# Window attention with keys on partitions and a mask table after exp, ahead of a routed expert layer

## The chip, the cores and the metric

The kernel runs on one core of one Trainium2 chip. The metric is device time in microseconds (us) of one execution; three runs of the kernel before gave 893.92, 901.37 and 901.82 us, a median of 901.37 us. One execution was also recorded by the hardware profiler. Its rows name the engines: PE is TensorE's matmuls, PEld its weight loads, DVE VectorE, ACT ScalarE, POOL GpSimd, SP SyncE; a q behind a name means the engine's own queue, as it issues a DMA. L310 is line 310 of the kernel.

## What is computed

```python
# attention: q, k, v are (4 batches, 8 heads, 768 tokens, 64), n_global = 8, n_local = 96
scores = (1 / 8) * q @ k.T                       # per batch and head
rel = pos[:, None] - pos[None, :]
is_global = pos[None, :] < n_global
is_local = (rel >= 0) & (rel < n_local)
dist = where(is_global & ~is_local, n_local, abs(rel))
scores = where(is_global | is_local, scores - slope[h] * dist, -1e9)
a = exp(scores - max(scores)); a = a / (sum(a) + 1e-9)
x = concat_heads(a @ v)                          # (3072 tokens, 512)
# router and experts: 8 experts, w1 (512, 1024), w2 (1024, 512)
logits = normalised(x) @ normalised(expert_emb).T / tau
e = argmax(logits); gate = softmax(logits)[e]
out = gate * (relu(x @ w1[e]) @ w2[e])           # each token by its one expert
```

A query sees the 96 keys up to itself and the first 8 keys of the sequence. Each token goes to one expert. All data are float32.

## The kernel before

The kernel has two stages. `window_attention` (L256) computes attention and routes tokens; then a loop over the eight experts (L616) gathers each expert's tokens from DRAM, runs two matmul layers over up to 512 token slots and scatters the result to the output.

Before attention, `load_numbers` (L62) reads n_global and n_local and forms a flag that says whether the window fits. `values_load` (L606) brings it to the engines' registers and a `tc.If` chooses between `window_attention` and `dense_attention`. `window_bias` (L203) builds on DVE a bias for each head: minus slope times distance for a kept key, -1e9 for another.

Attention works on units: a pair of heads (2a, 2a + 1) and two tiles of 128 queries, 48 units in all. For each pair of heads `load` (L268) issues six DMAs for q, k and v on SP's queue, two pairs ahead, and POOL copies v into `vb`, whose first 32 rows are the sequence's first values (L278, L279). `prep` (L285) transposes six tiles of q and six of k (L291) and copies them to `qT` and `kT`. Then

- `score` (L303) multiplies with queries stationary, 64 rows deep (one head on partitions 0 to 63, the other on 64 to 127), 256 keys moving (L310). DVE scales and adds the bias (L315) and takes the maximum (L321); ACT computes exp with the maximum taken off and sums it (L326).
- `turn` (L329) transposes the weights (L336), so that keys lie on partitions, and ACT copies them out (L338).
- `attend` (L341) multiplies with the weights stationary, 128 by 128, and 64 columns of values moving (L348, L350). DVE divides by the sum (L352 to L354).

In the loop at L377 the score of unit i stands beside the turn of unit i - 1 and the attend of unit i - 2. The program is handed to a scheduler that orders each engine's instructions, so neighbouring steps can stand in one another.

When a batch's last unit is attended, `finish` (L359) writes its x to DRAM and calls `route` (L126) for six tiles of 128 tokens: squares for the norm (L131), four transposes per tile (L140), a copy (L142), four matmuls of 8 columns against the expert embedding (L145), and for the whole batch the choice of the expert, the gate and each token's slot (L149 to L192), then six indirect DMAs on POOL that scatter token number and gate into `meta` (L194). All six write the same tensor, so each waits for the one before. The weights of the first two experts are loaded after batch 0.

`expert` (L492) loads its slots (L495), gathers token rows by indirect DMA (L502), transposes them (L508) and multiplies (L517, L524). `overflow` (L534) handles an expert with more than 512 tokens; here it has nothing to do.

Of the kernel before, what the change touches and what calls it, by code (L numbers as in the profile page):

```python
# [9 lines left out]
F32 = mybir.dt.float32  # L10
# [6 lines left out]
P = 128  # L17
NEG = 1e9
GR = 32  # rows of a "before" key block that hold the sequence's first keys instead
CAP = 512  # token slots of one pass through an expert  # L20
# [6 lines left out]
def build_consts(k):  # L27
    nc, pool = k.nc, k.const
    k.ident = pool.tile([P, P], F32, name="ident")
    make_identity(nc, k.ident[:])  # L30

    # prefix[k, m] = 1 where k < m
# [4 lines left out]
    k.ones = pool.tile([P, P], F32, name="ones")  # L37
    nc.vector.memset(k.ones[:], 1.0)
    k.half = pool.tile([P, k.NT], F32, name="half")
    nc.vector.memset(k.half[:], 0.5)  # L40

# [7 lines left out]
    nc.vector.memset(k.cnt[:], 0.0)  # L49

    # A slot that no token takes names the row of zeros behind the last token, with gate 0.
    cols = k.E * k.N // P
    fill = k.setup.tile([P, cols, 2], F32, name="fill")
    nc.vector.memset(fill[:, :, 0], float(k.N))
    nc.vector.memset(fill[:, :, 1], 0.0)
    nc.scalar.dma_start(k.meta[:].rearrange("(p c) w -> p c w", p=P), fill[:])
    zrow = k.setup.tile([1, k.DM], F32, name="zrow")
    nc.vector.memset(zrow[:], 0.0)
    nc.scalar.dma_start(k.x_dram[k.N : k.N + 1, :], zrow[:])


def load_numbers(k, n_global, n_local):  # L62
    """n_global and n_local as float32 on every partition, and whether the windowed path holds."""
    nc, pool = k.nc, k.const
    raw = pool.tile([P, 2, 2], I32, name="raw")
    for i, ap in enumerate((n_global, n_local)):
        nc.sync.dma_start(raw[:, i, :], ap.bitcast(I32).partition_broadcast(P))
# [9 lines left out]

    ok = pool.tile([P, 3], F32, name="ok")
    nc.vector.tensor_scalar(out=ok[:, 0:1], in0=k.ng, scalar1=float(GR), scalar2=None, op0=ALU.is_le)
    nc.vector.tensor_scalar(out=ok[:, 1:2], in0=k.nl, scalar1=float(P - GR + 1), scalar2=None,  # L80
                            op0=ALU.is_le)
    nc.vector.tensor_scalar(out=ok[:, 2:3], in0=k.nl, scalar1=1.0, scalar2=None, op0=ALU.is_ge)
    flag = pool.tile([P, 1], F32, name="flag")
    nc.vector.tensor_reduce(out=flag[:], in_=ok[:], op=ALU.min, axis=AX.X)
    k.flag_i = pool.tile([P, 1], I32, name="flag_i")
    nc.vector.tensor_copy(out=k.flag_i[:], in_=flag[:])


def prep_expert_emb(k, emb_in, tau):
# [27 lines left out]
def new_weights(k):  # L117
    w1 = k.wp.tile([P, k.NC, k.F], F32, name="w1t", tag="w1t")
    w2 = k.wp.tile([P, k.NF, k.DM], F32, name="w2t", tag="w2t")
    return w1, w2  # L120


# [1 line left out]


def route(k, b, xb, pool):  # L126
# [525 lines left out]
```

## Time and profile before

| what | value |
|---|---|
| median of three runs | 901.37 us |
| span of the profiled execution, first to last instruction | 891.9 us |
| PE busy | 776.3 us, 87% of the span |
| PEld, DVE, ACT, POOL busy | 465.0, 243.8, 233.6, 130.4 us |
| first score matmul | 22.52 us |
| last block of attention normalised | 344.29 us |
| first expert matmul | 412.16 us |
| moved by DMA | 74.31 MB |
| granted TensorE clock, mean | 0.894 of 2.4 GHz |

The profiled execution's span is 9.5 us below the median of the runs. Busy time is the time in which an engine has an instruction in hand; matmuls overlap, and their ends are modelled, so records close behind each other share time. A float32 matmul call shows as two records, a transpose as one. Times of rows count from the span's start.

### The profile page before, as it was taken

Reading aid. Unit: us, or ns where it says so; the run is one execution under the profiler, and the core shown is the slowest. Engines: PE = TensorE matmul, PEld = TensorE weight load, DVE = VectorE, ACT = ScalarE, POOL = GpSimd, SP = SyncE. Lnnn points to the kernel's source line nnn. Section 1 sums busy time; section 2 is a strip of 40 time slices with the busy share of each in tenths; the row PEclk is TensorE's granted clock in tenths of the full one; section 3 lists DMA queues with packets and bytes.
Section 4 is the critical chain, followed back from the end, with each engine's and each line's share of the span. In section 5 each row is a group of like instructions: output and inputs, shape, how many; then the busy total and the mean of one; then the engine's idle time right before and its main releaser. Section 6 shows DMA issues by size and latency. Waiting matters only on the chain. (4 is left out here: it accounts for less than half of the span.)

```text
span 891.9 us, 8302 instructions
## 1 busy us (share of the span) xinstructions
PE 776.3 (87%) x3092; PEld 465.0 (52%) x3092; DVE 243.8 (27%) x562; ACT 233.6 (26%) x623; POOL 130.4 (15%) x153
## 2 busy tenths in 40 slices
PE   1899899899998997307999999999999999999993
PEld 1777687677776776303444444444444444444441
DVE  7676256624562672201011020010100101102000
ACT  1677356824573565000100001001010010000100
POOL 3110102210221020014012020020110101101000
PEclk9999569955896797556999999999999999999998
DMA  7796514531332001004114231342142412300000
GB/s 148 189 244 187 133 36 72 104 74 36 64 62 89 19 1 72 3 1 118 48 75 151 101 110 53 118 155 105 31 141 102 141 32 113 126 12 33 1 17 17
DMA packets 98498, 74.31 MB, mean 83 GB/s; under 512 B 79362, under 2 KB 79490, under 8 KB 98450
## 3 DMA queue, kind: packets, MB, share of 16 engines
q1 hardware_dynamic: 89248, 52.47, 22.1%
q0 software_dynamic: 5888, 14.71, 4.7%
q10 hardware_dynamic: 3314, 6.51, 2.0%
q8 instruction: 27, 0.44, 0.2%
q14 instruction: 21, 0.17, 0.1%
HBM read 60.87 MB, written 14.90 MB: 85 GB/s over the span
## 5 line engine op out<-in xcount | busy, mean ns | idle before, releaser
L517 PE MATMUL big<-xT,w1t 128*128 128x512 f32 x512 | 223.5, 597 | 11.2 <-DVE xT L509 10.4
L524 PE MATMUL work<-w2t,hT 128*128 128x512 f32 x512 | 221.0, 592 | 0.0
L517 PEld LDWEIGHTS big<-xT,w1t 128*128 128x128 f32 x512 | 97.3, 191 | 132.8 <-issue 120.8
L524 PEld LDWEIGHTS work<-w2t,hT 128*128 128x128 f32 x512 | 97.3, 190 | 122.5 <-issue 122.5
L519 ACT ACTIVATE hT<-big 128x1024 f32<-128x1024 f32 x32 | 32.8, 1024 | 450.8 <-PE big L517 450.8
L527 DVE TENSOR_SCALAR y<-work,emt 128x512 f32<-128x512 f32 x32 | 24.0, 750 | 385.8 <-PE work L524 385.8
L326 ACT ACTIVATE ex<-sc,nm 128x256 f32<-128x256 f32 x192 | 95.2, 499 | 15.2 <-DVE nm L321 15.1
L310 PE MATMUL big<-kT,qT 64*128 64x256 f32 x384 | 88.5, 497 | 11.4 <-DVE kT L301 9.6
L528 POOL DMA_INDIRECT out_dram<-y,ids x32 | 32.0, 1000 | 336.3 <-DVE y L527 328.6
L350 PE MATMUL work<-v,pt 128*128 128x64 f32 x384 | 74.4, 284 | 0.0
L336 PE MATMUL work<-ident,ex 128*128 128x128 f32 x352 | 66.3, 304 | 7.1 <-ACT ex L326 6.7
L315 DVE SCALAR_TENSOR_TENSOR sc<-big,bias 128x1024 f32<-128x1024 f32 x48 | 58.5, 1218 | 37.8 <-PE big L310 37.8
L348 PE MATMUL work<-vb,pt 128*128 128x64 f32 x320 | 63.4, 282 | 0.0
L350 PEld LDWEIGHTS work<-v,pt 128*128 128x128 f32 x384 | 61.2, 205 | 0.0
L338 ACT COPY pt<-work 128x512 f32<-128x512 f32 (+1 forms) x96 | 51.0, 549 | 38.9 <-PE work L336 38.0
L310 PEld LDWEIGHTS big<-kT,qT 64*128 64x128 f32 x384 | 45.4, 225 | 29.0 <-issue 19.5
L336 PEld LDWEIGHTS work<-ident,ex 128*128 128x128 f32 x352 | 43.5, 157 | 30.6 <-ACT ex L326 24.2
L321 DVE TENSOR_REDUCE nm<-sc 128x4 f32<-128x1024 f32 x48 | 58.3, 1215 | 0.4
L145 PE MATMUL work<-en,xt 128*128 128x8 f32 x192 | 43.2, 354 | 17.1 <-ACT xt L142 16.2
L145 PEld LDWEIGHTS work<-en,xt 128*128 128x128 f32 x192 | 41.0, 315 | 29.9 <-ACT xt L142 28.4
L348 PEld LDWEIGHTS work<-vb,pt 128*128 128x128 f32 x320 | 51.9, 204 | 1.0 <-ACT pt L338 1.0
L194 POOL DMA_INDIRECT meta<-mt,slot x24 | 23.7, 986 | 184.6 <-DVE slot L191 111.7
(110 smaller groups left out, 443.6 us busy)
## 6 DMA issues: line engine op xcount, KB each, us to landing
w1t<-in_moe_w_dram SPq DMA_DIRECT2D x8, 2048.0 KB
w2t<-in_moe_w_dram SPq DMA_DIRECT2D x8, 2048.0 KB, 10.3
q<-in_q_dram SPq DMA_DIRECT2D x32, 192.0 KB, 3.3
k<-in_k_dram SPq DMA_DIRECT2D x32, 192.0 KB, 5.2
v<-in_v_dram SPq DMA_DIRECT2D x32, 192.0 KB, 2.8
x_dram<-xb ACTq DMA_DIRECT2D x4, 1536.0 KB
xg<-x_dram,ids POOLq DMA_INDIRECT x32, 3.6
out_dram<-y,ids POOLq DMA_INDIRECT x32, 2.7
```

The lines of the kernel that those rows point to most:

```text
L145: nc.tensor.matmul(lp[:, 0:E], lhsT=xt[:, c, :], rhs=k.en[:, c, :], start=c == 0, stop=c == k.NC - 1)
L310: nc.tensor.matmul(sp[:, e, r, :], lhsT=t.qT[rows, 2 * g + r, :], rhs=t.kT[rows, 2 * g + r, :, :].rearrange("p i c -> p (i c)"), start=Tru ...
L315: nc.vector.scalar_tensor_tensor(out=sc[:].rearrange("p e r c -> p e (r c)"), in0=sp[:].rearrange("p e r c -> p e (r c)"), scalar=k.scale, ...
L321: nc.vector.tensor_reduce(out=nm[:], in_=sc[:], op=ALU.max, axis=AX.X, negate=True)
L326: nc.scalar.activation(u.ex[:, e, r, :], sc[:, e, r, :], AF.Exp, bias=nm[:, e, r : r + 1], accum_out=u.den[:, r, e : e + 1])
L336: nc.tensor.transpose(ps[:, i, :], u.ex[:, e, i // 2, (i % 2) * P : (i % 2 + 1) * P], k.ident[:])
L338: nc.scalar.copy(out=pt[:, first:4, :], in_=ps[:, first:4, :])
L348: nc.tensor.matmul(av[:, r, e, 0:D], lhsT=u.pts[e][:, 2 * r, :], rhs=t.vb[:, qt - 1, e, :], start=True, stop=False)
L350: nc.tensor.matmul(av[:, r, e, 0:D], lhsT=u.pts[e][:, 2 * r + 1, :], rhs=t.v[:, qt, e, :], start=qt == 0, stop=True)
L517: nc.tensor.matmul(ps[:, i, :], lhsT=w1[:, c, f * P : (f + 1) * P], rhs=xT[:, c, :], start=c == 0, stop=c == k.NC - 1)
L519: nc.scalar.activation(hT[:, 2 * f2 : 2 * f2 + 2, :], ps[:], AF.Relu)
L524: nc.tensor.matmul(ps[:], lhsT=hT[:, f, j * P : (j + 1) * P], rhs=w2[:, f, :], start=f == 0, stop=f == k.NF - 1)
```

## The change

The change replaces attention and the router's matmuls. It has these parts.

1. **Units.** A unit is now four heads (a group has two pairs of heads), one block of 96 keys, and the 192 queries that can see it (96 for the last block). There are 8 groups of 8 units. Keys are stationary: `kT[:, j]` holds block j's 96 keys and 30 first keys of the sequence, so scores come out with keys on partitions, 126 rows.
2. **No maximum, no bias.** ACT computes exp straight from PSUM. DVE multiplies the result by a table that holds exp(-slope x distance) for kept keys and 0 for others. `window_table` builds it once.
3. **Values stationary.** `attend` multiplies with 64 columns of values stationary (two heads on two halves of the output's partitions) and the weights moving; four more calls with 32 columns of ones give the sums, one head on each quarter of the output's partitions. Two blocks of keys add up in PSUM; after four blocks DVE and ACT copy three banks out (`xd`).
4. **Router from the transposed result.** `sums` multiplies `xd` by the expert embedding, 32 columns wide, and transposes logits and sums; `rows` transposes x back, scales it, stores each tile of 128 tokens on SP's queue and squares it. Both are tasks, one per unit (two near the end), that run among the next units. `choose` is the rest of the old `route`.
5. **Order and memory.** The flag and the `tc.If` at the start are gone. q, k and v are loaded two groups ahead; the first group's q goes through ACT's queue. PSUM holds one score tile, four accumulators and two banks for transposes. Only the first expert's weights are loaded during attention, the second's when attention's memory is free.
6. **Fallback at the end.** Each batch checks that its reciprocal sums lie in a range; `leftover` runs the dense path at the end where that or the fit fails. It also does what `overflow` did.

```diff
-    with tc.If(fits > 0) as arm:
+    load_numbers(n, n_global, n_local)
+    build_consts(n)
+    with ExitStack() as moe:
+        wp_a = moe.enter_context(tc.tile_pool(name="wp_a", bufs=1))
+        n.w = [new_weights(n, wp_a)]
         with ExitStack() as inner:
             window_attention(n, inner)
...
+    sp_p, od_p, tp_p = (pool("wa_sp", 1, space=PSUM), pool("wa_od", 4, space=PSUM),
+                        pool("wa_tp", 2, space=PSUM))
+    qk_p, v_p, kt_p = pool("wa_qk", 4), pool("wa_v", 3), pool("wa_kt", 4)
...
+    def turn(t, i):
+        src, half = (t.k, t.q)[i // 2], i % 2
+        ps = bank()
+        for r in range(3):
+            nc.tensor.transpose(ps[:, r * P : (r + 1) * P], src[:, 3 * half + r, :, :], k.ident[:])
...
+        if i == 1:
+            nc.gpsimd.tensor_copy(out=t.kT[:, :, BLK:ROWS],
+                                  in_=t.kT[:, 0:1, 0:GLB].to_broadcast([P, NB, GLB]))
...
+    def score(u):
+        for a in range(2):
+            t = u.g.pairs[a]
+            for e in range(2):
+                rows = slice(e * D, (e + 1) * D)
+                nc.tensor.matmul(sp[0:ROWS, e, a * n : (a + 1) * n], lhsT=t.kT[rows, j, 0:ROWS],
+                                 rhs=t.qT[rows, j * BLK : j * BLK + n], start=True, stop=True)
+        nc.scalar.activation(ex, sp[0:ROWS, :, 0 : 2 * n], AF.Exp, scale=k.scale)
+        for e in range(2):
...
+            nc.vector.tensor_tensor(out=exv, in0=exv, in1=tb, op=ALU.mult)
...
+    def attend(u):
+        for od, at, c0, c1, first in parts:
+            cols = slice(at, at + c1 - c0)
+            for a in range(2):
+                for e in range(2):
+                    nc.tensor.matmul(od[a][e * D : (e + 1) * D, cols], lhsT=g.v[0:ROWS, 2 * a + e, j, :],
+                                     rhs=ex[:, e, a * n + c0 : a * n + c1], start=first, stop=True,
+                                     skip_group_check=True)
+            for a in range(2):
+                for e in range(2):
+                    i = 2 * a + e
+                    nc.tensor.matmul(od[2][32 * i : 32 * i + 32, cols], lhsT=k.ones[0:ROWS, 0:32],
+                                     rhs=ex[:, e, a * n + c0 : a * n + c1], start=first, stop=True,
+                                     skip_group_check=True)
...
+    def sums(t, i):
+            for a in range(4):
+                nc.tensor.matmul(ps[32 * a : 32 * a + 32, 3 * P : 4 * P], lhsT=k.enb[:, a, :],
+                                 rhs=xd[a // 2][:, a % 2, c], start=True, stop=True)
+            for m in range(2):
+                nc.tensor.transpose(ps[:, m * P : (m + 1) * P], xd[m][:, 2, c], k.ident[:])
+        if i > 0:
+            nc.tensor.transpose(ps[:, 2 * P : 3 * P], t.lS[i - 1][:], k.ident[:])
...
+    def rows(t, i):
+        for a in range(4):
+            nc.tensor.transpose(ps[:, a * P : (a + 1) * P], t.groups[a // 2].xd[i // 3][:, a % 2, c], k.ident[:])
+        nc.vector.tensor_tensor(out=xs[:], in0=ps[:].rearrange("p (h d) -> p h d", d=D),
+                                in1=t.rd[:, i, :].unsqueeze(2).broadcast_to([P, H, D]), op=ALU.mult)
+        nc.sync.dma_start(k.x_dram[r0 : r0 + P, :], flat)
+        nc.scalar.activation(sq[:], flat, AF.Square, accum_out=t.ss[:, i : i + 1])
...
+    LAG = 1
+    for i in range(len(units) + LAG):
+            if u.j == 0:
+                if gi + 2 < len(groups):
+                    load(groups[gi + 2])
...
+            score(u)
+            if gi + 1 < len(groups):
+                turn(groups[gi + 1].pairs[u.j // 4], u.j % 4)
+        last = i >= len(units) - 5
+        for _ in range(2 if last else 1):
+            if tasks:
+                tasks.pop(0)()
+        if i >= LAG:
+            u = units[i - LAG]
+            attend(u)
```

## Rows read from the trace of the kernel before

**Rows 1.** windows, us: length, PE PEld DVE ACT POOL busy (records), clock, DMA share, GB/s

```profile
22.00:87.00 65.00, 59.53 (x435) 47.43 (x436) 45.17 (x78) 46.43 (x143) 10.53 (x15) 1.00 0.77 211
87.00:116.00 29.00, 25.57 (x109) 19.53 (x109) 8.41 (x21) 11.00 (x32) 3.46 (x4) 0.57 0.47 109
...
299.00:345.00 46.00, 42.96 (x330) 35.54 (x326) 28.79 (x75) 33.54 (x105) 8.03 (x9) 1.00 0.05 10
345.00:412.00 67.00, 21.24 (x88) 17.57 (x88) 9.67 (x49) 4.98 (x11) 14.15 (x15) 0.52 0.15 48
412.00:880.00 468.00, 455.45 (x1136) 207.21 (x1136) 41.68 (x66) 32.77 (x32) 55.89 (x57) 1.00 0.23 82
```

**Rows 2.** costliest groups by line: records, busy us, mean ns, idle before

```profile
L310 PE MATMUL big<-kT,qT 64*128 64x256 f32 x384 | 88.5, 497 | 11.4 <-DVE kT L301 9.6 <-ACT qT L294 1.9
L350 PE MATMUL work<-v,pt 128*128 128x64 f32 x384 | 74.4, 284 | 0.0
```

**Rows 3.** order of time on PE, 43 to 48 us: start, length, line, records

```profile
43.19 0.82 PE L291 MATMUL big<-ident,k 128*128 128x128 f32 x6
44.24 1.13 PE L310 MATMUL big<-kT,qT 64*128 64x256 f32 x8 [0.23 <-ACT qT L294]
45.30 1.34 PE L336 MATMUL work<-ident,ex 128*128 128x128 f32 x8
...
46.88 0.61 PE L350 MATMUL work<-v,pt 128*128 128x64 f32 x4
47.33 0.39 PE L348 MATMUL work<-vb,pt 128*128 128x64 f32 x2
```

**Rows 4.** order of time, the last expert's second layer on PE

```profile
864.55 13.47 PE L524 MATMUL work<-w2t,hT 128*128 128x512 f32 x31
```

**Rows 5.** order of time, the start: first q load, first scores

```profile
7.16 0.97 SPq L273 DMA_DIRECT2D q<-in_q_dram  x2
...
22.52 3.79 PE L310 MATMUL big<-kT,qT 64*128 64x256 f32 x16 [8.20 <-DVE kT L301]
```

**Rows 6.** order of time on PE while batch 0 is routed, 99 to 105 us

```profile
99.71 1.85 PE L145 MATMUL work<-en,xt 128*128 128x8 f32 x8
101.41 1.09 PE L140 MATMUL work<-ident,xb 128*128 128x128 f32 x4
102.44 1.23 PE L310 MATMUL big<-kT,qT 64*128 64x256 f32 x4
103.59 1.87 PE L145 MATMUL work<-en,xt 128*128 128x8 f32 x8
```

**Rows 7.** order of time, from the last block of attention to the first expert

```profile
344.29 0.42 DVE L354 TENSOR_TENSOR xb<-work,den 128x256 f32<-128x256 f32 x1 [1.53 <-PE work L350]
...
366.54 0.17 DVE L147 COPY lg<-work 128x8 f32<-128x8 f32 x1 [3.39 <-PE work L145]
...
372.89 1.04 POOL L194 DMA_INDIRECT meta<-mt,slot  x1 [24.94 <-DVE slot L191]
...
399.78 1.30 SPq L495 DMA_DIRECT2D emt<-meta  x3
...
412.16 3.60 PE L517 MATMUL big<-xT,w1t 128*128 128x512 f32 x4 [0.78 <-issue]
```

**Rows 8.** groups by line again, and one row of the waits

```profile
L338 ACT COPY pt<-work 128x384 f32<-128x384 f32 x32 | 15.1, 477 | 15.1 <-PE work L336 15.1
...
L294 ACT COPY qT<-big 128x768 f32<-128x768 f32 x16 | 12.8, 798 | 39.1 <-PE big L291 39.1
...
L251 DVE TENSOR_TENSOR dist<-here,rel 128x256 f32<-128x256 f32 x1 | 0.4, 420 | 0.0
...
POOL meta L194 <- DMA meta<-mt,slot: 66.1, 16, 6.2
```

More of the change, by code (lines that the diff above doesn't have):

```diff
@@ L18 @@
 NEG = 1e9
-GR = 32
 CAP = 512
+BLK = 96
+GLB = 30
+ROWS = BLK + GLB
+NB = 8
+QB = 4
+RD_LO, RD_HI = 2.0**-64, 2.0**40
 class Net:
@@ L30, in build_consts, with build_route_consts @@
     make_identity(nc, k.ident[:])
+    k.ones = pool.tile([P, P], F32, name="ones")
+    nc.vector.memset(k.ones[:], 1.0)
+def build_route_consts(k):
+    nc, pool = k.nc, k.const
     k.prefix = pool.tile([P, P], F32, name="prefix")
@@ L104, in prep_expert_emb @@
     k.en = pool.tile([P, k.NC, E], F32, name="en")
-    ps = k.work.tile([P, 512], F32, name="work", tag="work")
     for c in range(k.NC):
@@ L108, in prep_expert_emb @@
     nc.vector.tensor_copy(out=k.en[:].rearrange("p c e -> p (c e)"), in_=ps[:, 0 : k.NC * E])
+    k.enb = pool.tile([P, k.NC, 32], F32, name="enb")
+    nc.gpsimd.memset(k.enb[:], 0.0)
+    for e in range(2):
+        rows = slice(e * k.D, (e + 1) * k.D)
+        nc.gpsimd.tensor_copy(out=k.enb[rows, :, e * E : (e + 1) * E], in_=k.en[rows])
 def load_weights(k, e, w):
@@ L134, in route @@
     nc.vector.reciprocal(out=ss[:], in_=ss[:])
-    lg = pool.tile([P, NT, E], F32, name="lg", tag="lg")
-    for t in range(NT):
-        tp = k.work.tile([P, 512], F32, name="work", tag="work")
-        for c in range(k.NC):
-            nc.tensor.transpose(tp[:, c * P : (c + 1) * P], xb[:, t, c * P : (c + 1) * P], k.ident[:])
-        xt = pool.tile([P, k.NC, P], F32, name="xt", tag="xt")
-        nc.scalar.copy(out=xt[:].rearrange("p c n -> p (c n)"), in_=tp[:])
-        lp = k.work.tile([P, 512], F32, name="work", tag="work")
-        for c in range(k.NC):
-            nc.tensor.matmul(lp[:, 0:E], lhsT=xt[:, c, :], rhs=k.en[:, c, :],
-                             start=c == 0, stop=c == k.NC - 1)
-        nc.vector.tensor_copy(out=lg[:, t, :], in_=lp[:, 0:E])
     m = pool.tile([P, NT], F32, name="m", tag="m")
@@ L173, in route @@
     nc.vector.tensor_copy(out=mt[:, :, 0], in_=k.tokid[:, b * NT : (b + 1) * NT])
-    cp = k.work.tile([P, 512], F32, name="work", tag="work")
     n = NT * E
@@ new lines, in leftover @@
+    passes = -(-k.N // CAP)
+    more = passes - 1
+    flags = k.const.tile([P, 2], F32, name="flags")
+    ps = k.work.tile([P, 512], F32, name="work", tag="work")
+    nc.vector.tensor_tensor(out=k.good[:], in0=k.good[:], in1=k.fits[:], op=ALU.mult)
+    nc.tensor.matmul(ps[:, 0:1], lhsT=k.ones[:], rhs=k.good[:], start=True, stop=True)
+    nc.vector.tensor_scalar(out=flags[:, 0:1], in0=ps[:, 0:1], scalar1=float(P), scalar2=None,
+                            op0=ALU.is_lt)
+    most = k.const.tile([P, 1], F32, name="most")
@@ L614 @@
[L614 to L623 removed]
+        n.work = ctx.enter_context(tc.tile_pool(name="work", bufs=4, space=PSUM))
+        n.big = ctx.enter_context(tc.tile_pool(name="big", bufs=2, space=PSUM))
@@ L627 @@
+        wp_b = moe.enter_context(tc.tile_pool(name="wp_b", bufs=1))
+        expert_pools(n, moe)
+        for e in range(n.E):
+            if e > 0:
+                w = new_weights(n, (wp_a, wp_b)[e % 2])
+                load_weights(n, e, w)
+            else:
+                w = n.w[0]
+            expert(n, n.meta[e * n.N : e * n.N + CAP, :], *w)
+    leftover(n)
 _INS = ['q', 'k', 'v', 'n_global', 'n_local', 'moe_expert_emb', 'moe_tau', 'moe_w1', 'moe_w2']
```

510 lines of the change are left out of this document (270 added, 240 removed).

## The prediction

> **What bounds the kernel now.** I read the stretches first, then the groups of instructions, then the order of TensorE's work inside one unit, and last the two ends of attention. The stretches [rows 1] show a first part (to 345 us) in which PE is nearly always busy, a gap (345 to 412 us: PE 21 of 67 us), and the experts (412 to 880 us: PE 455 of 468 us). The diff leaves `expert` alone, so whatever the change is worth lies ahead of 412.16 us, where the first expert matmul starts [rows 7].
>
> Attention has two faces. In 22 to 87 and 299 to 345 us the clock is at its upper level of 2.4 GHz and PE is busy 92 and 93% of the time. In 87 to 116 us, where batch 0 is routed, the granted clock is 0.57 and only 109 matmul records fit in 29 us, against 435 in the 65 us before [rows 1]. That pattern comes once per batch. In it PE runs eight router records of 8 columns, four transposes, four score records, over and over, one tile per 3.9 us [rows 6]: the next batch's scores wait their turn behind the router.
>
> The groups [rows 2] say on what a unit (two heads, two query tiles) spends PE: scores (L310), transposes of the weights (L336), and weights times values with the weights stationary and only 64 columns moving (L348, L350). Those last run at 0.11 us a record (four records of L350 from 46.88 us, the next at 47.33) [rows 3], held by the weight load, not by the columns. ACT and DVE are close behind: 46.4 and 45.2 of the 65 us from 22 to 87 [rows 1].
>
> **The price of a column.** Each float32 matmul call is two records (192 calls of L310, 384 records). 31 records of L524, 512 columns each, take 13.47 us [rows 4], 0.43 us apiece, so 0.84 ns per column and record: 192 columns 0.16 us, 128 columns 0.107 us. Six transposes take 0.82 us to the end of the last, whose own length is 0.27 us: 0.11 us each [rows 3].
>
> Eight score records of 256 columns would be 1.72 us in a row, but the next work starts 1.06 us after them (44.24 to 45.30) [rows 3]. So the head on partitions 0 to 63 and the one on 64 to 127 run in pairs (4 x 0.215 = 0.86 us), and 0.2 us is left, which I charge to every change of the tile's shape.
>
> **The change, unit by unit.** 64 units now (four heads, 96 keys plus 30 global ones, 192 query columns; the last of each eight has 96). PE per full unit:
> - scores, four calls: pairs as before, 4 x 0.16 + 0.2 = 0.84 us;
> - three transposes of q or k: 0.33 us;
> - values stationary, 64 wide, heads on output partitions 0 to 63 and 64 to 127: 4 x 0.16 + 0.2 = 0.84 us if they pair, 8 x 0.16 + 0.2 = 1.49 us if not;
> - sums with 32 columns of ones, on four quarters of the output partitions: 2 x 0.16 + 0.2 = 0.52 us if four go together, 1.49 us if not.
>
> No matmul of before has a stationary operand narrower than 128, so those two prices are bounds. I take the paired one: the nearest row is the score pair, the same engine and type split along the other side. A full unit is then 2.53 us (4.15 not paired), a half one 1.73 (2.53). 56 + 8 units: 155 us (253); the unit that crosses two accumulators splits its calls, 8 x 0.4 = 3 us more. What goes: all of L336 and of L348/L350.
>
> *The Trainium skill (TensorEngine Tiling, Key Properties) says that different tiles load and multiply in parallel and that changing the tiling mode drains the engine. The score pairs agree for rows (1.06 us instead of 1.72); for columns no run here shows it. By that rule the sum is the paired one, without it the other.*
>
> The router becomes `sums` and `rows`: per tile four calls of 128 columns, 32 wide (0.21 + 0.2 us paired, 1.06 not), and seven transposes (0.77 us): 1.18 us (1.83). 21 of 24 tiles lie among units: 25 us (38). PE sums to 155 + 3 + 25 = 183 us (294); at the 93% of rows 1 that is 197 us (316).
>
> **What hides the rest.** ACT per unit: one exp of 768 columns, as L294's 0.80 us, and one 384-column copy, 0.48 us [rows 8]; with squares and evacuations some 115 us. DVE: two multiplies of 384 columns; 0.42 us for 256 [rows 8] gives about 0.56 each; with evacuations, reciprocals and scaling some 140 us. Both lie under PE's 197 us; without that cover DVE would be next. The score tile has one buffer, so the next scores wait for the exp (0.8 us); PE has transposes and the unit before (1.7 us) meanwhile. Score, exp and multiply end 3.2 us after a unit starts and its `attend` comes one unit later, so the loop can't go below some 2.1 us a unit. Loads of q, k, v (96 of 192 KB) are the same 18.9 MB; at the 211 GB/s of 22 to 87 us [rows 1] that is 89 us, still hidden. Their SP queue now also holds the row stores, which wait for DVE; two groups of prefetch cover that.
>
> **Start.** The first q load is issued at 7.16 us behind the flag's branch and the first scores run at 22.5 us [rows 5]. The branch goes, so loads leave at about 1 us; four k and q tiles, 1.57 MB, need 7.4 us at that rate; then eight copies of 0.48 us and eight table exps of the same size on ACT. I put the first unit at 16 us (13 to 22). The first 16 score records took 3.79 us [rows 5], against 1.06 for eight later: a slow beginning, 4 us.
>
> **A wait moved.** A batch's six scatters take 372.89 to 399.78 us, 27 us, each waiting on POOL for the one before (16 such waits, 66.1 us) [rows 7, 8]. The next groups' global key copies, which scores need, now stand in that same queue, as do the value copies. A group lasts some 22 us. I charge 3 us for each of three batches, 9 us; bounds 0 and 15 each. In the unpaired case a group is longer and I charge 0.
>
> **Tail.** From the last normalised block (344.29) to the first scatter (372.89) are 28.6 us [rows 7], because six tiles are routed after it. Now three are: evacuation 0.6, three tiles at 1.8 (ACT and DVE in turn), the last sums and check 2.5, then the ranks, 6.3 as from 366.54 to 372.89: about 16 us. Scatters, ids, gathers and transposes to 412.16 stay: 39.3 us. The second expert's weights now load after attention, but the first expert's 58 us cover 4.2 MB (20 us). The check at the end: 2 us.
>
> **Sum.** Last `attend` at 16 + 4 + 197 + 9 = 226 us; first expert matmul at 226 + 16 + 39.3 = 281 instead of 412.16: 131 us earlier, 129 with the end. The profiled execution's span is 891.9 us, 9.5 below the median of the runs, 901.37; I carry that difference along: 762 us of span, 772 us.
>
> **Rivals.**
> 1. Column tiles don't pair: attention ends at 16 + 4 + 316 = 336 us, experts start at 391, 19 us gained with the end: 882 us. For it: no row shows a narrow tile. Against: rows pair in the same data type.
> 2. Something between: two go together but not four, or one routed stretch per batch still runs at the lower level, or POOL's scatters hold a group for 10 to 15 us. One of these is 30 to 60 us: about 820 us.
> 3. The other side: TensorE stays at 1.2 GHz. It fell there at each router, when it ran many small records that wait for copies [rows 1, 6], and the new stream has small tiles everywhere. Then 183 us become 366, 394 at 93%; attention ends at 423, experts start at 478, 68 us late with the end: 969 us. It is slower than before once attention ends after 355 us, that is, when about two thirds of it run at the lower level. Against: moving parts of 96 columns and more in place of 8, and the units of before, with 64, ran at the upper level.
> 4. The check sends it to the dense path. With scores of order 0.1 the sums lie between about 1 and 126, far inside the bounds, and n_local 96 and n_global 8 fit. Under 1 in 100; the dense path would cost more than attention does now.
>
> *The Trainium skill (TensorE: Matmul & The Clock Gate, "Why this matters for your kernels") warns of idle gaps between bursts as what takes the clock down. Rows 1 differ: 25.6 of 29 us busy at 0.57. By that rule alone rival 3 would need stalls; by the rows it would not.*
>
> **How the numbers follow.** Forecast, with pairs: 0.61, own range 735 to 805 us. Rival 2: 0.22. Rival 1: 0.11. Rival 3, and rival 1 with part of its time at the lower level: 0.06. Three runs of before spread from 893.92 to 901.82 us, so under 1% can't be told from no change. Faster by over 1%: 0.91; within 1%: 0.03 (rival 1 with a little more waiting); slower: 0.06. The range goes from the floor of 2.1 us a unit (about 35 us below, 735) to the unpaired sum, 882; it leaves out rival 3 and some of rival 1.
>
> **What would show it.** Right: pairs of attend records starting together, unit period near 2.8 us, upper level from about 20 us to the last `attend`, experts starting near 280 us and as long as before, no L336. Wrong: narrow records 0.16 us apart one by one; clock 0.5 in the stretches with `sums`; PE waiting for the key copies on POOL; a tail longer than 55 us.

## The result, and the profile after

The changed kernel takes 800.36 us, median of 4 runs (797.95 to 800.97), against 900.28 us (893.92 to 901.82) for the kernel before on the same chip: a ratio of 0.893, 95% interval 0.887 to 0.900. Forecast were 772 us in a range of 735 to 882. Direction and mechanism came out; of the 129 us forecast, 100 came.

The profiled execution spans 798.2 us. Its attention in stretches, with the units' holes cut out as stretches of their own (columns as in [rows 1]):

```profile
16.00:30.00 14.00, 12.07 (x62) 7.56 (x64) 3.30 (x7) 7.69 (x16) 2.70 (x3) 1.00 1.30 221
30.00:43.00 13.00, 12.66 (x148) 7.64 (x148) 7.93 (x14) 4.70 (x8) 1.96 (x1) 1.00 0.85 143
43.00:54.00 11.00, 7.79 (x65) 5.29 (x65) 2.70 (x8) 4.85 (x11) 3.68 (x8) 0.84 0.54 114
54.00:106.00 52.00, 51.65 (x574) 32.44 (x572) 28.66 (x68) 26.07 (x56) 4.99 (x7) 1.00 0.82 203
106.00:119.00 13.00, 10.07 (x70) 5.97 (x66) 8.71 (x36) 3.04 (x6) 2.58 (x2) 0.74 0.61 119
119.00:154.00 35.00, 35.00 (x399) 22.32 (x395) 18.38 (x45) 17.75 (x38) 5.00 (x5) 1.00 1.05 107
154.00:182.00 28.00, 15.31 (x132) 9.43 (x128) 10.53 (x37) 6.83 (x15) 8.16 (x8) 0.76 0.47 73
182.00:248.20 66.20, 66.13 (x757) 41.77 (x749) 41.55 (x137) 31.16 (x68) 11.75 (x13) 1.00 0.12 34
248.20:316.40 68.20, 10.55 (x66) 6.83 (x63) 12.47 (x57) 3.15 (x11) 17.28 (x18) 0.57 0.34 100
316.40:784.50 468.10, 456.81 (x1138) 208.04 (x1138) 41.77 (x67) 32.75 (x32) 54.59 (x56) 0.99 0.23 82
```

Read it in three parts. Between the holes PE is busy 52 of 52, 35 of 35 and 66 of 66 us, at the upper level: there the units run at about their price. The holes (43 to 54, 106 to 119, 154 to 182 us) have a PE with 8, 10 and 15 busy microseconds. The experts take 468 us, as in [rows 1]. The first expert matmul comes at 316.40 us instead of 412.16 [rows 7]; nearly all of the gain is ahead of it.

PE's order of time over a unit without tasks (start, length, line, records; compare [rows 3]):

```profile
29.77 0.87 PE L359 MATMUL od<-ex,v 126*64 126x192 f32 x8
30.57 0.53 PE L365 MATMUL od<-ex,ones 126*32 126x192 f32 x8
31.04 0.92 PE L329 MATMUL sp<-qT,kT 64*126 64x192 f32 x8
31.89 0.87 PE L359 MATMUL od<-ex,v 126*64 126x192 f32 x8
```

From start to start: values 0.80 us, sums 0.47, scores 0.85, where the prediction had 0.84, 0.52 and 0.84. The groups and waits that answer to [rows 2, 8]:

```profile
L339 DVE TENSOR_TENSOR ex<-ex,table 126x384 f32<-126x384 f32 (+1 forms) x128 | 67.9, 568 | 94.9 <-ACT ex L333 94.9
L329 PE MATMUL sp<-qT,kT 64*126 64x192 f32 (+1 forms) x512 | 67.8, 363 | 18.4 <-POOL kT L318 16.4 <-ACT qT L316 1.9
```

```profile
POOL meta L196 <- DMA meta<-mt,slot: 106.9, 20, 9.6
PE sp L329 <- POOL kT L318: 16.4, 3, 6.5
DVE ss L149 <- POOL ss L148: 12.0, 2, 10.8
POOL emb_ss L114 <- ACT emb_sq L113: 8.2, 1, 8.2
```

In all four POOL is the engine waited for or the one that waits; the waits of scatters on one another grew from 66.1 us [rows 8] to 106.9. Of the three waits of L329 one, 4.92 us, stands ahead of the first unit; the other two, 5.02 and 6.46 us, are in the third hole. Where the first hole comes from, in order of time:

```profile
36.08 0.29 SPq L110 DMA_DIRECT2D emb<-in_moe_expert_emb_dram  x1
...
44.52 0.48 ACT L372 COPY xd<-od 128x384 f32<-128x384 f32 x1 [1.94 <-PE od L359]
44.90 0.62 ACT L113 ACTIVATE emb_sq<-emb 8x512 f32<-8x512 f32 x1
45.70 0.58 POOL L114 TENSOR_TENSOR emb_ss<-emb_ss,half 8x1 f32<-8x1 f32 x1 [8.21 <-ACT emb_sq L113]
...
48.89 1.68 POOL L302 COPY v<-v 30x1792 f32<-30x1792 f32 x1
...
50.63 0.38 POOL L318 COPY kT<-kT 128x240 f32<-128x240 f32 x1
...
51.44 1.01 PE L329 MATMUL sp<-qT,kT 64*126 64x192 f32 x4
```

POOL stands 8.21 us for the square of the experts' embedding; the value copy and the key copy stand behind it, and the scores behind these. The embedding's load is issued late on SP's queue, but the square doesn't wait for it: in the trace the load's eight packets of 2 KB end at 38.43 us. The square stands in ACT's order behind a copy of the accumulators, which waits for PE. And the third hole, on POOL and then on PE:

```profile
161.08 0.96 POOL L196 DMA_INDIRECT meta<-mt,slot  x1 [5.80 <-DMA meta<-mt,slot]
162.05 0.39 POOL L318 COPY kT<-kT 128x240 f32<-128x240 f32 x1
167.78 1.67 POOL L302 COPY v<-v 30x1792 f32<-30x1792 f32 x1 [5.35 <-issue]
169.52 0.39 POOL L318 COPY kT<-kT 128x240 f32<-128x240 f32 x1
```

```profile
162.49 1.01 PE L329 MATMUL sp<-qT,kT 64*126 64x192 f32 x4 [5.02 <-POOL kT L318]
169.96 1.01 PE L329 MATMUL sp<-qT,kT 64*126 64x192 f32 x4 [6.46 <-POOL kT L318]
```

The first key copy starts as the last scatter of batch 0 leaves POOL, the second behind a value copy that itself stood 5.35 us; the scores follow each within 0.1 us. The profile names no releaser for these 5.35 us ("issue"), but the trace's semaphores do: until 167.62 us POOL's queue waits on the semaphore that the last scatter raises, and the scatter's last piece lands at 167.59. It is so in all eleven traces with early scatters: this value copy, of the seventh group, starts 0.1 to 0.2 us after batch 0's last scatter has landed. So the scatters hold POOL's queue until the last one has landed, not only until it is issued. Why the program has the copy wait for it, no run shows. The tail, from the last `attend` to the first expert:

```profile
247.78 0.37 PE L365 MATMUL od<-ex,ones 126*32 126x96 f32 x8
...
258.18 0.63 ACT L430 ACTIVATE sq<-xs 128x512 f32<-128x512 f32 x1 [3.71 <-DVE xs L424]
...
268.60 0.96 POOL L196 DMA_INDIRECT meta<-mt,slot  x1 [4.15 <-DMA meta<-mt,slot]
269.58 1.36 POOL L148 TENSOR_TENSOR ss<-ss,half 128x6 f32<-128x6 f32 x1
270.97 0.17 DVE L149 TENSOR_SCALAR ss<-ss 128x6 f32<-128x6 f32 x1 [10.78 <-POOL ss L148]
...
274.44 1.03 POOL L196 DMA_INDIRECT meta<-mt,slot  x1 [3.51 <-DVE slot L193]
```

The last square is done at 258.9 us, but the power that follows it stands on POOL behind batch 2's scatters, until 269.58.

### The profile page after: what moved, and what is told of

The parts are those of the page before. It is cut to its first block, busy times and chain, and to the rows that moved or that the text cites. A ratio compares the mean times of both kernels' runs of the same rounds, so it can differ in the third digit from the quotient of the medians.

```text
span 798.2 us, 8386 instructions
## 1 busy us (share of the span) xinstructions
PE 682.1 (85%) x3390; PEld 350.2 (44%) x3390; DVE 180.6 (23%) x488; ACT 141.6 (18%) x263; POOL 120.0 (15%) x141
## 4 chain that ended last, share of the span: by engine, by line
PE 62%; DMA 8%; DVE 5%; issue 2%; POOL 1%; ACT 0%; DVEq 0%; POOLq 0%
PE big L638 28%; PE work L645 28%; DMA meta<-mt,slot 7%; DVE xT L630 2%; PE sp L329 2%; PE od L359 2%; PE tp L311 1%; PE od L365 1%; DVE y L648 1%; DVE ex L339 0%; DMA xg<-x_dram,ids 0%; PE tp L422 0%; DMA emt<-meta 0%; PE work L629 0%; PE tp L400 0%
## 5 line engine op out<-in xcount | busy, mean ns | idle before, releaser
L339 DVE TENSOR_TENSOR ex<-ex,table 126x384 f32<-126x384 f32 (+1 forms) x128 | 67.9, 568 | 94.9 <-ACT ex L333 94.9
L329 PE MATMUL sp<-qT,kT 64*126 64x192 f32 (+1 forms) x512 | 67.8, 363 | 18.4 <-POOL kT L318 16.4
L333 ACT ACTIVATE ex<-sp 126x768 f32<-126x768 f32 x64 | 49.1, 766 | 91.5 <-PE sp L329 75.6
L359 PE MATMUL od<-ex,v 126*64 126x192 f32 (+1 forms) x576 | 61.2, 321 | 2.8 <-DVE ex L339 2.8
L329 PEld LDWEIGHTS sp<-qT,kT 64*126 64x126 f32 x512 | 44.4, 196 | 39.0 <-POOL kT L318 17.7
L196 POOL DMA_INDIRECT meta<-mt,slot x24 | 24.2, 1007 | 137.7 <-DMA meta<-mt,slot 106.9
L623 POOL DMA_INDIRECT xg<-x_dram,ids x32 | 31.0, 967 | 83.8 <-issue 43.2
L359 PEld LDWEIGHTS od<-ex,v 126*64 126x64 f32 x576 | 33.9, 139 | 21.5 <-issue 12.1
L365 PE MATMUL od<-ex,ones 126*32 126x192 f32 (+1 forms) x576 | 35.9, 318 | 0.0
L630 DVE COPY xT<-work 128x512 f32<-128x512 f32 x32 | 20.1, 683 | 7.1 <-PE work L629 7.1
L311 PE MATMUL tp<-ident,q 128*128 128x128 f32 x96 | 19.8, 325 | 1.0 <-DMA q<-in_q_dram 1.0
```

Of the source, the lines that this page charges most:

```text
L311: nc.tensor.transpose(ps[:, r * P : (r + 1) * P], src[:, 3 * half + r, :, :], k.ident[:])
L329: nc.tensor.matmul(sp[0:ROWS, e, a * n : (a + 1) * n], lhsT=t.kT[rows, j, 0:ROWS], rhs=t.qT[rows, j * BLK : j * BLK + n], start=True, stop ...
L333: nc.scalar.activation(ex, sp[0:ROWS, :, 0 : 2 * n], AF.Exp, scale=k.scale)
L339: nc.vector.tensor_tensor(out=exv, in0=exv, in1=tb, op=ALU.mult)
L359: nc.tensor.matmul(od[a][e * D : (e + 1) * D, cols], lhsT=g.v[0:ROWS, 2 * a + e, j, :], rhs=ex[:, e, a * n + c0 : a * n + c1], start=first ...
L365: nc.tensor.matmul(od[2][32 * i : 32 * i + 32, cols], lhsT=k.ones[0:ROWS, 0:32], rhs=ex[:, e, a * n + c0 : a * n + c1], start=first, stop= ...
```

## The experiments

Theory A: PE's price per unit is as predicted, and the missing 28 us are waits that reach PE through POOL's queue (embedding, scatters, copies, power) and through DVE's order. Rivals: the price of the column tiles, the loop of exp and multiply, or the transfers themselves. The table has what the traces show: the second group's first unit to its second ("1"), the third unit of the fourth group to its fifth ("2"), the last unit of the fifth group to the seventh of the sixth ("3"), the end of the last `attend`, the first expert matmul, and the tail between these two. All times in us.

| kernel | first unit | 1 | 2 | 3 | last attend | tail | first expert | median | ratio, 95% interval |
|---|---|---|---|---|---|---|---|---|---|
| after, first | 15.9 | 10.0 | 12.3 | 37.6 | 248.2 | 68.2 | 316.4 | 800.36 | 0.893, 0.887-0.900 |
| e0 after again | 18.0 | 9.8 | 12.0 | 32.9 | 242.4 | 66.4 | 308.8 | 793.53 | 0.887, 0.882-0.893 |
| e1 key copy on DVE | 16.3 | 9.8 | 11.5 | 29.1 | 238.1 | 62.4 | 300.5 | 787.66 | 0.883, 0.877-0.888 |
| e2 power on ACT | 17.7 | 9.7 | 11.1 | 29.8 | 241.9 | 59.3 | 301.2 | 786.84 | 0.883, 0.877-0.889 |
| e4 embedding first | 14.1 | 2.1 | 11.8 | 29.3 | 230.7 | 65.3 | 296.0 | 779.62 | 0.873, 0.868-0.878 |
| e5 no early scatters | 17.9 | 9.7 | 11.6 | 25.9 | 237.5 | 54.8 | 292.3 | 772.52 | 0.865, 0.860-0.871 |
| e10 choose cut | 17.1 | 10.0 | 7.7 | 35.6 | 241.2 | 65.7 | 306.9 | 788.68 | 0.882, 0.877-0.887 |
| e11 four parts | 13.5 | 2.2 | 9.0 | 31.7 | 230.4 | 62.9 | 293.2 | 776.93 | 0.869, 0.865-0.874 |
| e12 four, all powers | 14.5 | 2.1 | 6.4 | 29.7 | 229.0 | 59.5 | 288.5 | 772.26 | 0.864, 0.858-0.869 |
| e9 e1 + e2 + e4 | 13.8 | 2.1 | 9.6 | 25.7 | 229.5 | 58.2 | 287.7 | 771.41 | 0.862, 0.856-0.867 |

The nearest to undisturbed values in these traces: 2.1 for 1 (e4), 6.4 for 2 (e12), and 22.2 for 3 (the same seven units one batch earlier in e12, 89.8 to 112.0 us).

**e0, the changed kernel again.**

> The changed kernel itself, once more, beside the experiments, so that they stand against it on the same chip. Its first time was 800.36 us at a ratio of 0.8933 to the kernel before; the same ratio within 0.01 is expected, 795-803 us.

793.53 us, as expected but for 1.5 us. Experiments are compared with it by their ratios to the kernel before, since the runs came from several chips (0.01 of ratio is 8.9 us).

**e8, the price of column tiles.**

```diff
+            nc.vector.memset(g.od[2][:], 1.0)
...
-                    nc.tensor.matmul(od[2][32 * i : 32 * i + 32, cols], lhsT=k.ones[0:ROWS, 0:32],
-                                     rhs=ex[:, e, a * n + c0 : a * n + c1], start=first, stop=True,
+                    nc.tensor.matmul(od[2][0:32, cols], lhsT=k.ones[0:ROWS, 0:32],
+                                     rhs=ex[:, e, a * n + c0 : a * n + c1], start=first and i == 0, stop=True,
```

> All four sums of ones of a unit (L365) are put on the same 32 partitions of the sums' tile instead of on four different quarters (the sums are then those of four heads together, the other three quarters hold the number 1, so the result is scaled otherwise; the number, shape and order of TensorE's records stay the same, and VectorE sets the tile to 1 first, 16 times about 0.4 us). Theory A (the prediction's price: four records on four column quarters run together, on the same columns they run one after the other): the eight records of a full unit take 8 x 0.16 = 1.29 us instead of 0.47 us, over some 60 units +45 to +50 us, about 848 us. Rival B (the sums lie beside the waits for exp and the table, TensorE has the room): 0 to +12 us. Rival C (the quarters do not run together, only the distance in the queue changed): no change in the 0.47 us.

The two kernels' sums and the scores behind them, e8 and then e0:

```profile
66.02 1.49 PE L367 MATMUL od<-ex,ones 126*32 126x192 f32 x8
67.44 0.92 PE L329 MATMUL sp<-qT,kT 64*126 64x192 f32 x8
```

```profile
60.24 0.53 PE L365 MATMUL od<-ex,ones 126*32 126x192 f32 x8
60.70 0.92 PE L329 MATMUL sp<-qT,kT 64*126 64x192 f32 x8
```

1.42 us instead of 0.46: on one quarter the eight run one after the other. The last `attend` ends at 288.3 instead of 242.4, 45.9 us later. Theory A; B and C fall. (The whole took 1157.70 us, which can't be compared: with these sums the routing differs, and more expert passes run behind the eight.)

**e6, the multiplies.**

```diff
-            nc.vector.tensor_tensor(out=exv, in0=exv, in1=tb, op=ALU.mult)
+            pass
```

> The multiplication of exp's result by the table (L339) is left out, 128 instructions and 62.9 us of VectorE; everything else, the table's making too, stays. The prediction cost these at nothing, hidden beside TensorE's units. Theory A (hidden where VectorE has nothing else, but the holes near 110 and 165 us are multiplies that stand behind other work on VectorE): -6 to -14 us against the changed kernel on the same chip, the units' distance elsewhere unchanged at 2.1 to 3.4 us. Rival B (a part of every unit's time is the chain score, exp, multiply, attend, one unit late): the units' distance falls everywhere, -20 us and more. Rival C (nothing): 0 to -3 us.

The last `attend` ends at 232.8, 9.6 us earlier than in e0, and the distances elsewhere stay (4.4, 3.0, 3.2 us behind the sixth unit of the second group in both): rival B falls. The amount is A's, but only stretch 2 (8.7 instead of 12.0) is its mechanism. In stretch 3 (24.7 instead of 32.9) the third to fifth units still take 6.7 and 2.7 us; what went there is the wait on the key copy, since batch 0's last scatter came at 142.8 us here and at 155.5 in e0. So DVE's 68 us are hidden, but for some 3 us beside `choose`, no more than rival C allowed. The total, 1092.12 us, has more expert passes again.

**e4, the embedding.** The first line stood in `prep_expert_emb`, the second ends `load_numbers`; tau's load moves with it.

```diff
-    nc.sync.dma_start(emb[:], emb_in[:, :])
+    nc.scalar.dma_start(k.emb[:], k.emb_in[:, :])
```

> The loads of tau and of the experts' embedding are issued at the beginning on ScalarE's queue, ahead of the attention's loads that follow there, instead of late on SyncE's; nothing else changes. Theory A (the hole of 43.4-53.4 us after comes from GpSimd standing 8.2 us at L114 for the square of an embedding that lands late, with the values' and the keys' copies behind it): the hole shrinks from 10 to about 3 us: -6 to -7 us, about 793.5 us. Rival B (the values and keys of that group are late by their own transfers, and GpSimd is only the last in the row): the hole stays to 2 us: -2 to 0 us; and +1 to +2 us if the two loads ahead delay the first unit.

More than expected, 0.0146 of ratio below e0, 13 us: stretch 1 falls from 9.8 to 2.1 us, the amount of theory A. Its "lands late" is not what happened, since in the first profile the load had landed 6 us before the square ran; with the load at the start the scheduler also orders the square ahead, to 8.10 us on ACT. The first unit comes 3.8 us earlier than in e0, 1.7 earlier than in the first profile. Attention ends 11.7 us earlier. In stretch 3 the wait on the key copy goes too, though nothing was done to it: batch 0's last scatter is issued at 147.32 us, when the group that needs the copy is only just due (lines are one higher here).

```profile
147.32 0.96 POOL L197 DMA_INDIRECT meta<-mt,slot  x1 [5.36 <-DMA meta<-mt,slot]
148.29 0.71 POOL L319 COPY kT<-kT 128x240 f32<-128x240 f32 x2
```

So whether the scatters hold a group is a matter of a few microseconds: this group starts 3.8 us after the unit before it, in the first profile 8.3, without a hold 3.2.

**e1, the key copy.**

```diff
-            nc.gpsimd.tensor_copy(out=t.kT[:, :, BLK:ROWS],
+            nc.vector.tensor_copy(out=t.kT[:, :, BLK:ROWS],
```

> The key copy (line 318, 16 of them) is issued on VectorE instead of GpSimd; nothing else changes. Theory A (GpSimd's queue is the missing term: the key copies stand behind the router's scatters, and TensorE's units wait for them): the waits of the scores on kT in the trace after (5.02 us near 162, 6.46 us near 170, 4.6 us near 50, together 16.4 us on L329) go, VectorE takes 16 x about 0.6 us more behind TensorE, and the last attend moves from 248 to 232-236: about -14 us, some 786 us, and the wait group of L329 on GpSimd is gone. Rival B (the holes come from TensorE's low clock after a fall, or from VectorE's own queue; the wait on kT is only the last of several): the holes stay, since the copy now stands behind VectorE's other work there: 0 to -4 us, 796-800 us.

A part of theory A. No score waits for POOL any more (of the 16.4 us expected to go, 4.92 stood at 15.87 us ahead of the first unit, none near 50), and the distances from 152.6 us on start with 3.2, 2.5, 2.7. But then one of 9.8 us comes: the hole moved to the third unit, where DVE stands 3.56 us for batch 1's power, which stands behind a value copy on POOL (held until batch 0's last scatter lands, at 160.78 us), and then beside the next value copy. Stretch 1 stays at 9.8: there PE's own transposes of the embedding wait 2.90 us in the chain, whoever copies the keys. By the ratios 4 us of theory A's 14, with intervals that overlap e0's.

**e2, the power.**

```diff
-    nc.gpsimd.tensor_tensor(out=ss[:], in0=ss[:], in1=k.half[:], op=ALU.pow)
+    nc.scalar.activation(ss[:], ss[:], AF.Sqrt)
```

> In choose() the power 0.5 on GpSimd becomes a Square Root on ScalarE, followed by the same addition on VectorE; nothing else changes. Theory A (the tail from the last attend to the first expert is longer than the kernel before's since batch 3's power stands behind batch 2's scatters on GpSimd): the wait of 10.78 us at 271 us goes, the first of batch 3's scatters still stands behind batch 2's last, which ends about 270, so the start of the scatters moves from 274.4 to at best 270 and less if the slots become the limit: only -4 to -5 us in the tail; and the hole at 106-114, where VectorE stood behind the power of batch 0, shrinks by up to 7 us. Together -5 to -11 us, 790-796 us. Rival B (the table loads that ScalarE needs around a square root, two of about 1.3 us per batch, and its place in ScalarE's queue eat that): -2 to +3 us, 798-804 us.

In the trace 7 us, all of it in the tail (66.4 to 59.3), next to none from stretch 2 (12.0 to 11.1): there the power alone wasn't the cause, as e10 shows below. Rival B's price is in the trace too. Stretch 3 is 3.1 us shorter than in e0, but the last `attend` comes only 0.5 us earlier: beside batch 2's square root ACT loads two tables, 1.28 us each, and the exp of the last group's second unit waits for them (the second load):

```profile
219.68 1.28 ACT L333 ACT_TABLE_LOAD   x1
```

That unit takes 5.6 us instead of 2.4; in e9 and e12 it takes 6.2 and 5.3. By the ratios 4 us, with overlapping intervals.

**e5, the scatters.**

```diff
-    for t in range(NT):
+    for t in range(NT if b == k.B - 1 else 0):
```

> The scatters of slots (L196) of batches 0 to 2 are left out, only batch 3's six remain; tokens of the first three batches get no slot, and the experts do the same amount of work on empty slots. Theory A (the scatters, one after the other on GpSimd at about 4 to 9 us each, are what holds the key copies at 154-174 us, 14 us, and what batch 3's power and first scatter wait for in the tail, 11 us): last attend at 232-236, tail 57-59 us instead of 68.2, together -22 to -26 us, about 776 us. Rival B (only the tail is held by them; the holes in the attention come from elsewhere): -9 to -12 us, about 790 us. Rival C (neither: the memory traffic of the outputs and of the experts' weights sets the tail, whatever GpSimd does): -14 us from the attention alone, given back in part, 786-795 us with a tail that stays over 65 us.

Theory A: stretch 3 is 7.0 us shorter than in e0 and 11.7 shorter than in the first profile, the last `attend` comes at 237.5 (1.5 us later than expected), and the tail falls to 54.8; by the ratios 20 us under e0, with intervals apart. Most of it is the tail, 11.6 us; in the attention the holes 1 and 2 stay. Rival C falls: the stores of x and the second expert's weights load as before, and the tail is short all the same.

**e10, `choose` in three tasks.** It becomes a generator with two yields, one ahead of the prefix matmuls and one behind their copy.

```diff
-        choose(k, t.b, t.lg, t.ss, rt_p, bank())
+        parts = choose(k, t.b, t.lg, t.ss, rt_p, bank)
+        for _ in range(2 if t.b < B - 2 else 0):
+            tasks.append(lambda: next(parts))
...
```

> choose() of batches 0 and 1 is cut in three tasks, one per unit (up to the first expert of the highest logit and the gate; the two matmuls with the prefix and their copy; ranks, slots and scatters), so that units of the attention stand between its parts on VectorE and on TensorE; the work is the same. Theory A (the holes of 106-118 us and a part of those of 162-174 us come from the table multiplies standing behind choose's chain on VectorE, and from TensorE's own prefix matmul standing in order behind that chain): the longest distance of two units there falls from 8.2 and 11.4 us to about 4-5 us, the fall to the low clock near 110 goes: -6 to -10 us, 790-794 us. Rival B (the time is the low clock's and the same work only moves by a unit; or the later scatters hold the key copies longer): -2 to +3 us.

Stretch 2 falls as theory A has it, from 8.0 + 4.0 to 4.7 + 3.0 us. At 152.5 us a unit of 16.2 us gives it back (three lines higher here; POOL, then PE):

```profile
156.60 0.98 POOL L199 DMA_INDIRECT meta<-mt,slot  x1 [4.14 <-DMA meta<-mt,slot]
162.79 1.68 POOL L305 COPY v<-v 30x1792 f32<-30x1792 f32 x1 [5.21 <-issue]
```

```profile
164.97 1.01 PE L332 MATMUL sp<-qT,kT 64*126 64x192 f32 x4 [11.86 <-POOL kT L321]
```

The units came 4 us earlier and met the same queue: last scatter, its landing (162.59 us), value copy, key copy. By the ratios 5 us in total, with overlapping intervals.

**e11, four parts together.**

> Four parts together: the key copy on VectorE, the embedding's loads first on ScalarE's queue, choose of batches 0 and 1 cut in three tasks, and the power of the last batch alone as a square root on ScalarE. If the theory holds that the missing time is waits on GpSimd's and VectorE's queues in the attention, and on GpSimd in the tail: last attend at 220-226 us (predicted for the change itself: 226), first expert matmul at 278-284, about 764-770 us, which is the predicted 772 for the change or a little under it. If the parts overlap (each takes away the same wait): not under 776 us, near the embedding's run alone (ratio 0.873).

Not reached: 776.93 us. The third unit of the sixth group still took 11.8 us. POOL and DVE there:

```profile
156.37 1.68 POOL L309 COPY v<-v 30x1792 f32<-30x1792 f32 x1 [6.71 <-issue]
158.13 1.36 POOL L152 TENSOR_TENSOR ss<-ss,half 128x6 f32<-128x6 f32 x1
159.53 0.17 DVE L153 TENSOR_SCALAR ss<-ss 128x6 f32<-128x6 f32 x1 [8.85 <-POOL ss L152]
159.61 1.02 DVE L346 TENSOR_TENSOR ex<-ex,table 126x384 f32<-126x384 f32 x2
```

A small addition at the head of DVE's queue waits 8.85 us for a power that stands behind a value copy; the multiplies that PE needs run right after it. The value copy in turn starts as batch 0's last scatter has landed (156.26 us), so the scatters stand behind this hold too. I had moved the power of the last batch only.

**e12 and e9, every power moved, with and without the cut.**

> As the four parts together, but the power of every batch is a square root on ScalarE, not of the last batch alone; nothing of the attention's path to VectorE's queue is left behind GpSimd then, except the values' copy. Theory A (the hole of 151-163 us that the four parts left is VectorE's addition in choose, standing 8.85 us behind a power that stands behind the values' copy on GpSimd, whose own values land late): that hole falls to 4-6 us, the last attend comes at 222-225 instead of 230.4, batch 2's scatters and the tail keep their 60-63 us: some 767-771 us, ratio 0.860-0.865. Rival B (the table loads around each square root and the exp after it cost 2 x 1.3 us in each of three batches in the middle of the attention): 774-778 us, no gain. Rival C (the hole is the late values themselves, whoever waits): the hole only moves to the next unit that needs them, 774-777 us.

> As the run before (key copy on VectorE, the embedding first, every power on ScalarE), but choose in one piece as in the changed kernel. Theory A (choose's chain of some 30 short operations on VectorE, with TensorE's prefix matmul in order behind it, is worth 3 to 4 us a batch by itself, as the cut alone showed at 106 us: 8.0 + 4.0 us became 4.7 + 3.0 us): 5 to 8 us slower than the run with the cut, 773-778 us. Rival B (once the power is off GpSimd the chain is hidden): within 2 us of it.

e12: the hole at the third unit is gone (3.8 us), but two units behind it take 5.4 and 9.0, and the last `attend` comes at 229.0, 1.4 us earlier than in e11: the hole only moved, as in rival C, but not for late values. At the first of the two units DVE waits for the landing of batch 0's last scatter (156.97 us), as the value copy on POOL does; then its copy of six columns takes 1.70 us beside that value copy (last section), with the multiplies behind it:

```profile
157.09 1.70 DVE L177 COPY mt<-tokid 128x6 f32<-128x6 f32 x1 [1.81 <-DMA meta<-mt,slot]
```

What set the second unit was not followed further; the next value copy ran beside it. The tail gained 3.4 us. The ratio, 0.864, is theory A's (0.860 to 0.865), but not by its way: it had the gain in the attention and the tail as in e11. The intervals overlap e11's. e9, without the cut, is as fast (771.41 against 772.26 us), so A falls for the cut and B holds. e9, three small edits, is the version to keep: its ratio lies 0.026 (23 us) below the changed kernel's, with intervals apart. A kernel with the root in the last batch alone, but without the cut, was not run.

## Why the prediction was right, and where its size was off

**The price of a unit: right.** 0.80, 0.47 and 0.85 us against 0.84, 0.52 and 0.84; e8 shows by 45.9 us that the four quarters do run together, and 0.80 us for eight value records of 0.16 us that the two halves do. That decides rival 1. *The rule of the Trainium skill (TensorEngine Tiling, Key Properties) that different tiles multiply in parallel holds for columns here: 0.46 us for eight records on four quarters, 1.42 us for the same eight on one.*

**The sum of the units: right, in part by luck.** The last `attend` came at 248.2 us, predicted 226. Take the first three units (12.4 us from the first start to the third, instead of 2 x 2.1) and the stretches 1 to 3 against their undisturbed values: 8.2 + 7.9 + 5.9 + 15.4 = 37.4 us of holes. What is left, 248.2 - 15.9 - 37.4 = 195 us, is close to the predicted 197. But 14 of the 197 us were idle time (183 us at 93%), and between the holes PE had next to none: 153 of 153 us busy. So the work itself took some 12 us more than the 183 priced. The eight units of the third group (74.17 to 100.77 us) keep PE busy for 26.2 us; by the prices they are 24.6. Three transposes cost 0.45 us there instead of 0.33, and `sums` and `rows` of a tile 1.37 instead of 1.18. Two errors of some 7% cancel.

**The waits: the mis-sized term.** I charged 4 us for the beginning and, under "A wait moved", "3 us for each of three batches, 9 us". Measured: 8.2, and 29.2 in its place. The mechanism that I named, key copies behind the scatters, is there, for one batch and not for three, and it cost about what I charged: 5.02 + 6.46 us of waits of PE in the third hole, and without the scatters (e5) stretch 3 is 7.0 to 11.7 us shorter. What I had at nothing is the rest. The embedding cost 7.9 us: the diff moved its load from ACT's queue at the start to SP's behind the attention's loads, and the scheduler its square with it (e4 took both back). Stretch 2 lost 5.9 us, before any scatter was issued: the power on POOL (a wait of 1.18 us), a multiply beside a value copy (last section), and `choose`'s chain in DVE's order with PE's prefix matmul in order behind it (4.3 us came back in e10). 3.7 us of stretch 3 stay in e5 as well. I had priced what the diff adds to attention and the router, and not gone through `prep_expert_emb`, which it touches too. Of the beginning only a part is explained: eight scores take 1.57 us there (24.45 to 26.02) against 0.85 later, and the trace's first record of the clock stands at 28.6 us, so the 1.00 in the first row of stretches doesn't say at which level they ran.

**The tail: mis-sized too.** Predicted 16 + 39.3; measured 26.3 to the first scatter (274.44 - 248.15) and 42.0 behind it. The 10 us are batch 2's scatters ahead of batch 3's power. In the kernel before POOL had stood idle for 24.94 us ahead of the first scatter [rows 7], so nothing of batch 2 was left there; I carried the row over without asking what is still on POOL when attention ends earlier. e5 shows the tail without them: 14.7 + 40.1 us, 54.8, which is the predicted 55.3. (The terms that I listed for the 16 add up to 14.8.)

**First unit, end.** 15.9 us for 16 (13.5 to 18.0 in the other traces): the number was right, the way to it another. I had put it behind loads and ACT's copies; it stands behind POOL, whose queue I had not counted:

```profile
15.37 0.91 POOL L318 COPY kT<-kT 128x240 f32<-128x240 f32 x2
15.87 1.00 PE L329 MATMUL sp<-qT,kT 64*126 64x192 f32 x2 [4.92 <-POOL kT L318]
```

That key copy comes after a value copy, which waited until 10.43 us for its load, and after the setup of constants and distances. The end (last scatter at 784.57 to 798.2) is 13.6 us, against 12.8 before (879.08 to 891.9): 0.8 us for the 2 charged.

**Sum.** 22 us late at the last `attend` and 13 in the tail make 35 at the first expert matmul (316.4 for 281). In time it is 28, since the median of the runs lay 2.2 us above the profile's span and not 9.5 as I carried along. The 9.5 was an error: an execution's time lies some 2 us above its span, so the profiled one of before was most likely the fastest of the three, 893.92 us. By luck it hid 7 of the 35 us. Two of my signs of being wrong are in the trace, PE waiting for key copies on POOL and a tail over 55 us; they marked sizes of terms, not the price of the units.

**Rivals.** Rival 2 named the right engine ("POOL's scatters hold a group for 10 to 15 us") and came nearest with 820. Rival 3, TensorE at 1.2 GHz, is out: the stretches of `sums` and `rows` ran at 1.00. In attention the clock fell three times, for 3.4, 6.8 and 13.7 us, each time behind a hole (at 49.1, 110.6 and 161.8 us); in e4, where the first hole is gone, that fall is gone too. *That is the warning of the Trainium skill (TensorE: Matmul & The Clock Gate, "Why this matters for your kernels") of idle gaps, which [rows 1, 6] had not shown: here it agrees.* Rival 4 didn't come: no line of the dense path is in the trace.

## What to carry to other kernels

When a faster engine pulls the end of a stage forward, list for each in-order queue everything that is still in it at that moment: here the sum of the new work was right to about 1% (in part by luck), and most of what was missing stood on POOL behind serial scatters and their landing, or in ACT's and DVE's order behind work of another stage. Where the profile gives a wait no releaser, ask what the queue waits for: the 4 to 7 us ahead of the seventh group's value copy were a scatter's landing. A tiny operation in such a queue (a power of 128x6, the square of an embedding) can hold the whole pipeline, and three short edits that moved such operations gave 23 us, nearly the whole miss. After each edit look at which queue the same units now meet: in e1, e10 and e11 a part of the gain went into the wait behind it.

## What I had not expected of the hardware

A copy on POOL stops a multiply on DVE. In the changed kernel's second hole (POOL's line and DVE's, order of time):

```profile
107.04 2.47 DVE L339 TENSOR_TENSOR ex<-ex,table 126x384 f32<-126x384 f32 x2
107.17 1.92 POOL L302 COPY v<-v 30x1792 f32<-30x1792 f32 x1 [0.52 <-DMA v<-in_v_dram]
```

The two multiplies take 2.47 us where two take 1.02 (e11's L346 above): the second, 2.03 us long by itself, starts while the copy runs and ends 0.4 us after it. In e12 even an addition of 8 columns, 0.17 us otherwise, took 1.63 us beside such a copy (POOL's line, then DVE's):

```profile
160.73 1.67 POOL L306 COPY v<-v 30x1792 f32<-30x1792 f32 x1 [1.97 <-PE od L363]
```

```profile
160.79 1.63 DVE L192 TENSOR_TENSOR cnt<-cnt,both 128x8 f32<-128x8 f32 x1
```

*The Trainium skill (SBUF — State Buffer, "SBUF: two separate sides") says that VectorE and GpSimd share a pair of ports as an exclusive lock, held for a whole instruction; these rows agree.* In the changed kernel four of the eight value copies meet such an instruction on DVE and add 1.2 to 1.5 us to it, on an engine that has room except inside the holes.

Scatters beside loads are slower: five steps of batch 0 from 119.51 to 161.08 us, 8.3 us each, against 5.0 for batch 3 (274.44 to 299.64). DMA engines were busier in the first stretch (share 1.05 from 119 to 154 us, 0.34 in the tail); that this is the reason is argued, not tried.
